# First three gated units by single row tile, in a fused layer-norm, spectral-filter and GEGLU kernel

## Chip, cores and metric

The kernel runs on one core of a Trainium2 chip. The time is the device time of one launch in microseconds (us), and the median of several runs counts; lower is better.

## Reference

```python
def _A_ref(x, w_r, w_i):                      # global spectral filter
    X = jnp.fft.rfft2(x.astype(jnp.float32), axes=(-2, -1))
    return jnp.fft.irfft2(X * (w_r + 1j * w_i), s=(S, D), axes=(-2, -1)).astype(jnp.bfloat16)

def _B_ref(x, w_gate, w_up, w_down):          # GEGLU, tanh gelu
    h = _gelu(x @ w_gate) * (x @ w_up)
    return h @ w_down

xn = _layernorm(A_x)                          # (1, 2048, 512) bf16, eps 1e-5
return A_x + _A_ref(xn, A_w_r, A_w_i) + _B_ref(xn, B_w_gate, B_w_up, B_w_down)
```

The gate and up weights are 512 x 1792, the down weights 1792 x 512, all bf16. The input B_x is not used.

## The kernel before

The 2048 rows are 16 tiles of 128 partitions; tile j holds the rows 16p + j. Four tiles make a block of 512 rows. Two branches share the normalized rows `xn`.

**The normalization.** `ln_stats(j)` (L410) takes the mean and variance of a tile on DVE (VectorE), in two instructions, statistics and aggregate. For the first two tiles `ln_sqrt` (L416) takes the root on ACT (ScalarE) and `ln_recip` (L420) the reciprocal on DVE; for the others `ln_rstd` (L425) does both on POOL (GpSimd). `ln_apply(j)` (L433) writes the normalized tile on DVE. Between tiles 0 and 1 nothing is split: one root and one reciprocal serve both.

**Transposes.** PE (TensorE) contracts over partitions, so the gated branch needs `xnT`, the rows transposed, in four chunks of 128 features. `transposes_by_tile(0, 2, ring_sp)` (L439) does the eight 128 x 128 transposes of tiles 0 and 1 and copies each chunk of 256 rows, in turn on DVE and ACT. `transposes` (L461) does two or four tiles at once in the same way; the last two blocks use DMA transposes (`transfers`, L488).

**The gated branch.** `geglu_unit(b, fc, a, w, ring)` (L529) makes 128 of the 1792 hidden features for w rows of block b from row a: four gate matmuls, four up matmuls, gelu on ACT out of the gate's PSUM bank, and the product on DVE out of the up bank into `hT`. There are 14 units to a block. Each unit takes two PSUM banks from a ring (`ring_first` has six, `ring_gu` three). A bank comes free when gelu or the product has read it. `down_unit` (L577) does the down projection of one tile.

The first units of block 0 are made in two passes: units 0 to NHALF - 1 for rows 0 to 255 first, then the same for rows 256 to 511; the rest have all 512 rows. All matmuls of one engine are in program order.

**The spectral branch** goes by `half_fold` (POOL, L500), `mirror_fold` (DVE, L507), `unit_A` and `unit_d` (PE, L610 and L636), a shuffle through DRAM, `unit_B`, the filter product on DVE, `unit_c`, a second shuffle, `unit_e` and `unit_fin`. Its small matmuls alternate with gated and down units, which the code calls fillers (`filler`, L838). They are taken from one list in a fixed order.

**Order.** There is no planner: `_Sched` (L152) records each operation on its engine's list in the order in which the Python code calls it, with semaphores for what it depends on. Every engine runs its list strictly in order. An instruction of DVE that waits holds all DVE instructions behind it.

**Loads.** SP and ACT issue the DMAs. The gate and up weights come in five column pieces (`WPIECES`, L344), loaded by `load_w` (L348). One semaphore counts both loads of a piece, and the gate matmuls wait for it. Up weights of piece 0 are issued by ACT after the identity; SP issues x tiles 0 and 1, the gate weights of piece 0, x tiles 2 and 3, pieces 1 and 2, and then the rest. `warm_up` (L519) runs matmuls on zeros at the start, 46 with no wait but that for the zeros, and 4 after the first reciprocal.

Of the kernel before, what the change touches and what calls it, by code (L numbers as in the profile page):

```python
# [7 lines left out]
ACT = mybir.ActivationFunctionType  # L8
# [6 lines left out]
HD = 256  # L15
NK = 257
FF = 1792
P = 128
NJ = 16
NG = 32  # L20
NDC = 4
NFC = 14
NGG = 3
NX1 = 4
NWARM = (46, 4)
LN_EPS = 1e-5


# [123 lines left out]
class _Sched:  # L152
# [14 lines left out]
    def total(self, stream):  # L167
        return (stream, self.stream_cnt[stream])
# [59 lines left out]
def bass_parallel_sum__spectral_gfnet__glu_gated_geglu__prompt_kernel(  # L228
# [15 lines left out]
    xv = A_x.rearrange("b (p j) d -> p (b j) d", j=NJ)  # L244
# [3 lines left out]
    sch = _Sched()  # L248

    with ExitStack() as es:  # L250
# [4 lines left out]
        x_sb = sb("x_sb", [P, NJ, D])  # L255
        xnT = sb("xnT", [P, NDC, S])
        wg_sb = sb("wg_sb", [P, NDC, FF])
        wu_sb = sb("wu_sb", [P, NDC, FF])
# [26 lines left out]
        xn = bufA[:, :].rearrange("p (j c) -> p j c", j=NJ)  # L285
# [12 lines left out]
        ident = small[:, 0:P]  # L298
# [20 lines left out]
        def sp_bank_bf(slot):  # L319
            return ps_bf[:, slot * 1024:(slot + 1) * 1024]  # L320
# [3 lines left out]
        ring_sp = _Ring((3, 4, 5, 6), bank_readers)  # L324
        ring_dn = _Ring((7,), bank_readers)

        ring_first = _Ring((0, 1, 2, 7, 5, 6), bank_readers)
        ring_tr = _Ring((3, 4), bank_readers)

        streams = [("pe", 1), ("act", 1), ("dve", 1), ("pool", 1)]  # L330
        streams += [(n, 16) for n in ("x0", "x1", "x2", "x3", "xc1", "xc2", "xc3", "ident", "small", "fa", "eg", "wd", "wr", "wi",
                                      "w0", "w1", "w2", "w3", "w4", "dr0", "dr1", "perm1", "jx0", "jx1", "jx2", "jx3", "vd0_0", "vd0_1", "vd0_2", "vd1_0", "vd1_1", "vd1_2", "vd2_0", "vd2_1", "vd2_2", "vd3_0", "vd3_1", "vd3_2", "perm2", "tr2", "tr3", "out")]
        for name, inc in streams:
            sem = es.enter_context(nc.semaphore("sem_" + name))
            sch.add_stream(name, sem, inc)
        total = sch.total

        def load(stream, dst, src, eng="sp"):
            sch.op(eng, lambda e: e.dma_start(dst, src), stream=stream)
            return total(stream)  # L340


        ev_id = load("ident", small[:, 0:P], c_small.ap()[:, 0:P], eng="act")
        WPIECES = ((0, 384), (384, 640), (640, 896), (896, 1280), (1280, FF))  # L344
        ev_w = {}
        spec = {}

        def load_w(i, which=(0, 1), eng="sp"):  # L348
            a, b = WPIECES[i]
            for q in which:  # L350
                dst, src = ((wg_sb, B_w_gate), (wu_sb, B_w_up))[q]
                load("w%d" % i, dst[:, :, a:b], src[:, a:b].rearrange("(r p) f -> p r f", p=P), eng=eng)
            ev_w[i] = total("w%d" % i)

        def load_xc(m):
            ev = load("xc%d" % m, x_sb[:, 4 * m:4 * m + 4, :], xv[:, 4 * m:4 * m + 4, :])
# [1 line left out]
                ev_x[j] = ev  # L358

        ev_x = {}  # L360
        load_w(0, (1,), eng="act")
        for j in range(4):
            ev_x[j] = load("x%d" % j, x_sb[:, j, :], xv[:, j, :])
            if j == 1:
                load_w(0, (0,))
        load_w(1)
        load_w(2)
        load_xc(1)
# [41 lines left out]
        def ln_stats(j):  # L410
            ev = sch.op("dve", lambda e: e.bn_stats(st[:, j, :], x_sb[:, j, :]), deps=[ev_x[j]])  # L411
            ev_ag[j] = sch.op("dve", lambda e: e.bn_aggr(ag[:, j, :], st[:, j, :]), deps=[ev])  # L412
# [3 lines left out]
        def ln_sqrt(a, b):  # L416
            return sch.op("act", lambda e: e.activation(rstd[:, a:b], ag[:, a:b, 1], ACT.Sqrt, bias=eps_t[:], scale=1.0),
                          deps=[ev_ag[b - 1], ev_eps])

        def ln_recip(a, b, ev):  # L420
            ev = sch.op("dve", lambda e: e.reciprocal(rstd[:, a:b], rstd[:, a:b]), deps=[ev])
            for j in range(a, b):
                ev_rstd[j] = ev
# [7 lines left out]
        ev_xn = {}  # L431

        def ln_apply(j):  # L433
            ev_xn[j] = sch.op("dve", lambda e: e.tensor_scalar(xn[:, j, :], x_sb[:, j, :], ag[:, j, 0:1], rstd[:, j:j + 1],  # L434
                                                             ALU.subtract, ALU.mult), deps=[ev_rstd[j], ev_ag[j]])

        ev_xnT = {}

        def transposes_by_tile(a, b, ring):  # L439

            n = (b - a) * P
            slots = [ring.alloc(1) for _ in range(NDC)]
            banks = [sp_bank_bf(slot)[:, 0:n] for slot, _ in slots]
            evs = []
            for j in range(a, b):
                for r in range(NDC):
                    ev_t = sch.op("pe", lambda e, j=j, r=r: e.transpose(banks[r][:, (j - a) * P:(j - a + 1) * P], xn[:, j, r * P:(r + 1) * P], ident),
                                  deps=[ev_id, ev_xn[j]] + slots[r][1])
                    if j < b - 1:
                        continue  # L450
                    dst = xnT[:, r, a * P:b * P]
                    if r % 2 == 0:
                        ev = sch.op("dve", lambda e, dst=dst, r=r: e.tensor_copy(dst, banks[r]), deps=[ev_t])  # L453
                    else:
                        ev = sch.op("act", lambda e, dst=dst, r=r: e.activation(dst, banks[r], ACT.Copy), deps=[ev_t])
                    ring.add_reader(slots[r][0], ev)
                    evs.append(ev)
            for j in range(a, b):
                ev_xnT[j] = evs

        def transposes(a, b, ring, per=2):  # L461

# [66 lines left out]
        def geglu_unit(b, fc, a=0, w=512, ring=None):  # L529

            k = geg["k"]
            geg["k"] = k + 1
            s2 = k % NGG
            hb = b % 2
            ring = ring or ring_gu
            evw = [ev_w[i] for i, (lo, hi) in enumerate(WPIECES) if lo < (fc + 1) * P and fc * P < hi]
            evx = [ev_xnT[4 * b + i] for i in range(a // P, (a + w) // P)]
            gslot, gdeps = ring.alloc(1)

            def mm(e, wsb, slot, dcs=range(NDC)):  # L540
                ins = None
                for dc in dcs:
                    ins = e.matmul(gu_bank(slot)[:, 0:w], wsb[:, dc, fc * P:(fc + 1) * P], xnT[:, dc, b * 512 + a:b * 512 + a + w],  # L543
                                   start=(dc == 0), stop=(dc == NDC - 1))
                return ins

            if b == 0 and fc == 0 and a == 0:
                for dc in range(NDC):
                    ev_gm = sch.op("pe", lambda e, dc=dc: mm(e, wg_sb, gslot, (dc,)), deps=evw + [x[dc] for x in evx] + gdeps)
            else:  # L550
                ev_gm = sch.op("pe", lambda e: mm(e, wg_sb, gslot), deps=evw + evx + gdeps)
            uslot, udeps = ring.alloc(1)
            ev_um = sch.op("pe", lambda e: mm(e, wu_sb, uslot), deps=udeps)
            gg = gg_sb[s2][:, 0:w]
            ev_gg = sch.op("act", lambda e: e.activation(gg, gu_bank(gslot)[:, 0:w], ACT.Gelu_apprx_tanh),  # L555
                           deps=[ev_gm] + gg_readers[s2])
            gg_readers[s2] = []
            ring.add_reader(gslot, ev_gg)
            hdeps = []
            if fc == 0 and a == 0:  # L560
                hdeps = list(hT_readers[hb])
                hT_readers[hb] = []
            ev_h = sch.op("dve", lambda e: e.tensor_tensor(hT[hb][:, fc, a:a + w], gu_bank(uslot)[:, 0:w], gg, ALU.mult),  # L563
                          deps=[ev_um, ev_gg] + hdeps)
            ring.add_reader(uslot, ev_h)
            gg_readers[s2].append(ev_h)
            ev_h_block.setdefault(b, []).append(ev_h)
# [227 lines left out]
            finished(j, ev_o)  # L795


        NHALF = 6
        ln_stats(0)
        ln_stats(1)  # L800
        ev_sq = ln_sqrt(0, 2)
        sch.op("act", lambda e: e.activation(warm[:], eps_t[:], ACT.Gelu_apprx_tanh), deps=[ev_eps])
        ln_recip(0, 2, ev_sq)
        for n, ev in zip(NWARM, (None, ev_rstd[0])):
            warm_up(n, ev)
        ln_apply(0)
        ln_apply(1)
        transposes_by_tile(0, 2, ring_sp)
        ln_stats(2)
        ln_stats(3)  # L810
        ln_rstd(2, 4)
        for fc in range(NHALF):
            geglu_unit(0, fc, 0, 256, ring_first)
            if fc == 1:
                ln_apply(2)
                ln_apply(3)
                half_fold(0)
            if fc == 3:
                transposes(2, 4, ring_tr)
        for fc in range(NHALF):  # L820
            geglu_unit(0, fc, 256, 256, ring_first)
# [16 lines left out]
        def filler(n=1):  # L838
            for _ in range(n):
                u = next(fill, None)  # L840
                if u is None:
                    return
                todo["left"] -= 1
                if u[0] == "g":
                    geglu_unit(u[1], u[2])
                else:
                    down_unit(u[1], u[2])

        filler()
        for j in range(4, 8):  # L850
            ln_apply(j)
        filler(2)
        transposes(4, 8, ring_tr)
        half_fold(1)
        filter_i = load_filter("wi", wi_sb, A_w_i)
# [104 lines left out]
```

## Time and profile before

| | |
|---|---|
| runs (us) | 180.08, 180.95, 181.80; median 180.95 |
| profiled execution | 180.17 us, span 178.4 us |
| PE busy | 174.7 us (98%) |
| DVE, ACT, POOL busy | 116.0, 86.5, 55.2 us |
| DMA | 27.15 MB, mean 152 GB/s |
| first gate matmul | at 7.14 us |
| second pass of block 0 begins | at 12.97 us |
| transposes of tiles 4 to 7 begin | at 23.39 us |

The span is the time from the first to the last instruction in the trace; the rest of the execution's time lies around it. A matmul's recorded duration holds the way through the array, so matmuls in a row overlap, and it is their distance from start to start that counts. "Idle before" and "<-" name who ended a wait. "ps" is PSUM, "bufA" the normalized rows, "bufC" the half folds.

### The profile page before, as it was taken

Reading aid. Unit: us, or ns where it says so; the run is one execution under the profiler, and the core shown is the slowest. Engines: PE = TensorE matmul, PEld = TensorE weight load, DVE = VectorE, ACT = ScalarE, POOL = GpSimd, SP = SyncE. Lnnn points to the kernel's source line nnn. Section 1 sums busy time; section 2 is a strip of 40 time slices with the busy share of each in tenths; the row PEclk is TensorE's granted clock in tenths of the full one; section 3 lists DMA queues with packets and bytes.
Section 4 is the critical chain, followed back from the end, with each engine's and each line's share of the span. In section 5 each row is a group of like instructions: output and inputs, shape, how many; then the busy total and the mean of one; then the engine's idle time right before and its main releaser. Section 6 shows DMA issues by size and latency. Waiting matters only on the chain.

```text
span 178.4 us, 3133 instructions
## 1 busy us (share of the span) xinstructions
PE 174.7 (98%) x1136; PEld 98.2 (55%) x1136; DVE 116.0 (65%) x250; ACT 86.5 (49%) x159; POOL 55.2 (31%) x54
## 2 busy tenths in 40 slices
PE   7999999999999999999999999999999999999994
PEld 7888465555555544454555555444455555555443
DVE  3768958798685628438586785954355868885731
ACT  2644357777362633066375764632173536662100
POOL 0073290373630000000000000000017869997760
PEclk9999999999999999999999999999999999999999
DMA  4999999999998693913435666744500111111101
GB/s 147 323 342 379 372 379 149 202 156 239 221 159 198 150 313 106 324 53 81 123 104 125 123 184 149 177 90 117 118 6 29 59 59 32 61 65 48 41 29 59
DMA packets 37520, 27.15 MB, mean 152 GB/s; under 512 B 6656, under 2 KB 36736, under 8 KB 37376
## 3 DMA queue, kind: packets, MB, share of 16 engines
q1 hardware_dynamic: 33664, 24.95, 55.1%
q10 hardware_dynamic: 3840, 2.00, 5.8%
q8 instruction: 9, 0.15, 0.4%
q14 instruction: 7, 0.06, 0.2%
HBM read 17.48 MB, written 6.30 MB: 133 GB/s over the span
## 4 chain that ended last, share of the span: by engine, by line
PE 87%; POOL 5%; DVE 5%; issue 1%
PE ps L543 48%; PE ps L589 25%; POOL bufC L504 5%; PE ps L524 3%; PE ps L722 2%; PE ps L753 2%; PE ps L774 2%; PE ps L691 2%; DVE bufA L434 2%; DVE hT L563 1%; PE ps L616 1%; PE ps L642 1%; PE ps L473 1%; DVE bufB L509 1%; POOL rstd L427 1%
## 5 line engine op out<-in xcount | busy, mean ns | idle before, releaser
L543 PE MATMUL ps<-xnT,wg_sb 128*128 128x512 bf16 (+1 forms) x248 | 58.5, 359 | 0.3 <-DVE xnT L453 0.3
L543 PE MATMUL ps<-xnT,wu_sb 128*128 128x512 bf16 (+1 forms) x248 | 58.6, 359 | 0.0
L563 DVE TENSOR_TENSOR hT<-ps,gg 128x512 bf16<-128x512 f32 (+1 forms) x62 | 39.3, 637 | 23.2 <-PE ps L543 21.6
L589 PE MATMUL ps<-wd_sb,hT 128*128 128x512 bf16 (+2 forms) x238 | 50.7, 367 | 0.0
L555 ACT ACTIVATE gg<-ps 128x512 bf16<-128x512 f32 (+1 forms) x62 | 34.4, 555 | 25.2 <-PE ps L543 23.6
L788 POOL TENSOR_TENSOR bufC<-bufC 128x256 bf16<-128x256 f32 x16 | 14.7, 919 | 86.5 <-DVE bufC L785 86.5
L543 PEld LDWEIGHTS ps<-xnT,wu_sb 128*128 128x128 bf16 x248 | 24.2, 98 | 24.2
L589 PEld LDWEIGHTS ps<-wd_sb,hT 128*128 128x128 bf16 x238 | 22.4, 98 | 23.2
L543 PEld LDWEIGHTS ps<-xnT,wg_sb 128*128 128x128 bf16 x248 | 23.0, 98 | 15.4 <-issue 0.5
L600 DVE TENSOR_TENSOR x_sb<-ps,x_sb 128x512 bf16<-128x512 f32 (+2 forms) x17 | 11.2, 660 | 23.9 <-PE ps L589 23.9
L792 POOL TENSOR_TENSOR x_sb<-x_sb,bufC 128x512 bf16<-128x512 bf16 x16 | 18.7, 1169 | 2.3
L504 POOL TENSOR_TENSOR bufC<-bufA 128x1024 bf16<-128x1024 bf16 x8 | 16.8, 2124 | 7.9 <-DVE bufA L434 7.9
L758 ACT ACTIVATE bufA<-ps 128x512 bf16<-128x512 f32 x16 | 9.4, 597 | 16.9 <-PE ps L753 16.9
L727 ACT ACTIVATE Vp<-ps 128x514 bf16<-128x514 f32 x16 | 9.5, 599 | 15.4 <-PE ps L722 15.4
L650 ACT ACTIVATE bufB<-ps 128x512 bf16<-128x512 f32 x16 | 11.9, 743 | 9.5 <-PE ps L642 9.5
L411 DVE BATCH_NORM_STATS2 st<-x_sb 128x6 f32<-128x512 bf16 x16 | 10.9, 678 | 2.2 <-DMA x_sb<-in_A_x_dram 2.2
L784 DVE TENSOR_TENSOR bufC<-bufC,ps 128x256 f32<-128x256 f32 x16 | 6.7, 421 | 5.3 <-ACT bufC L781 5.3
L696 ACT ACTIVATE Xc<-ps 128x514 bf16<-128x514 f32 x12 | 7.0, 595 | 1.0 <-PE ps L691 1.0
L623 ACT ACTIVATE tmp<-ps 128x512 bf16<-128x512 f32 x9 | 5.4, 597 | 4.4 <-PE ps L616 4.4
L426 POOL TENSOR_SCALAR rstd<-ag 128x4 f32<-128x4 f32 (+1 forms) x4 | 1.3, 316 | 19.9 <-DVE ag L412 19.9
L781 ACT ACTIVATE bufC<-ps 128x256 f32<-128x256 f32 x16 | 6.0, 378 | 2.6 <-PE ps L774 2.6
L788 DVE TENSOR_TENSOR bufC<-bufC 128x256 bf16<-128x256 f32 x16 | 6.8, 425 | 0.5
(50 smaller groups left out, 138.0 us busy)
## 6 DMA issues: line engine op xcount, KB each, us to landing
stage_g<-Vp SPq DMA_DIRECT2D x16, 128.5 KB, 3.1
bufC<-stage_p SPq DMA_DIRECT2D x4, 512.0 KB, 5.5
out_dram<-x_sb SPq DMA_DIRECT2D x15, 128.0 KB, 1.8
wd_sb<-in_B_w_down_dram SPq DMA_DIRECT2D x1, 1792.0 KB, 14.8
stage_p<-bufB SPq DMA_DIRECT2D x7, 256.0 KB, 5.6
wr_sb<-in_A_w_r_dram SPq DMA_DIRECT2D x6, 257.0 KB, 10.8
wi_sb<-in_A_w_i_dram SPq DMA_DIRECT2D x6, 257.0 KB, 10.0
JX<-Xc SPq DMA_DIRECT2D x24, 64.2 KB, 2.3
```

What stands on the lines that cost most here:

```text
L411: ev = sch.op("dve", lambda e: e.bn_stats(st[:, j, :], x_sb[:, j, :]), deps=[ev_x[j]])
L504: ev_hf[m] = [sch.op("pool", lambda e, t=t, op=op: e.tensor_tensor(half[:, m, t, :, :], rows[:, 0, :, :], rows[:, 1, :, :], op), deps=deps ...
L543: ins = e.matmul(gu_bank(slot)[:, 0:w], wsb[:, dc, fc * P:(fc + 1) * P], xnT[:, dc, b * 512 + a:b * 512 + a + w], start=(dc == 0), stop=(d ...
L555: ev_gg = sch.op("act", lambda e: e.activation(gg, gu_bank(gslot)[:, 0:w], ACT.Gelu_apprx_tanh), deps=[ev_gm] + gg_readers[s2])
L563: ev_h = sch.op("dve", lambda e: e.tensor_tensor(hT[hb][:, fc, a:a + w], gu_bank(uslot)[:, 0:w], gg, ALU.mult), deps=[ev_um, ev_gg] + hdeps)
L589: ins = e.matmul(bank(slot)[:, 0:w], hT[hb][:, fc, jj * P:(jj + 1) * P], wd_sb[:, fc, cs], start=(fc == 0), stop=(fc == NFC - 1))
L600: ev_a = sch.op("dve", lambda e, slot=slot, cs=cs, w=w: e.tensor_tensor(x_sb[:, j, cs], bank(slot)[:, 0:w], x_sb[:, j, cs], ALU.add), deps ...
L650: ev_T[j] = sch.op("act", lambda e: e.activation(dst, src, ACT.Copy), deps=[ev_p])
L727: ev_v = sch.op("act", lambda e: e.activation(Vp[sv][:], sp_pair(slot), ACT.Copy), deps=[ev_p] + Vp_readers[sv])
L758: ev_ZT[j] = sch.op("act", lambda e: e.activation(ZT[:, :, j, :], src, ACT.Copy), deps=[ev_p] + [ev_xnT[i][0] for i in (11, 15)])
L788: y = [sch.op(("dve", "pool")[h], lambda e, h=h, op=op: e.tensor_tensor(rS[s2][:, h * HD:(h + 1) * HD], yeS[s2][:, 0, :], yeS[s2][:, 1, :] ...
L792: ev_o = sch.op("pool", lambda e: e.tensor_tensor(x_sb[:, j, :], x_sb[:, j, :], rS[s2], ALU.add), deps=[a, b, ev_xn[j]] + ev_acc.get(j, []))
```

## The change

The layer norm's root and reciprocal are taken for tile 0 and tile 1 apart. Tile 0 is transposed and copied on DVE (two pairs of chunks) before tile 1 is applied on DVE; tile 1 is transposed after unit 0 of tile 0 and copied on ACT. Units 0 to 2 are made for tile 0 alone, then for tile 1 alone; units 3 to 6 for both. The second pass has seven units. Gate and up weights have semaphores of their own, and up matmuls wait for theirs. Tile 1's load goes to ACT's queue, both loads of piece 0 to SP's ahead of tiles 2 and 3. The statistics of tiles 2 and 3 follow the products of the narrow units. There are 40 and 3 warm-up matmuls. One filler instead of two stands between the application of tiles 4 to 7 and their transposes.

```diff
-NWARM = (46, 4)
+NWARM = (40, 3)
...
+        streams += [("w%d%s" % (i, q), 16) for i in range(5) for q in "gu"]
...
-                load("w%d" % i, dst[:, :, a:b], src[:, a:b].rearrange("(r p) f -> p r f", p=P), eng=eng)
-            ev_w[i] = total("w%d" % i)
+                name = "w%d%s" % (i, "gu"[q])
+                load(name, dst[:, :, a:b], src[:, a:b].rearrange("(r p) f -> p r f", p=P), eng=eng)
+                ev_w[i, q] = total(name)
...
-        load_w(0, (1,), eng="act")
-        for j in range(4):
+        for j, eng in ((0, "sp"), (1, "act")):
+            ev_x[j] = load("x%d" % j, x_sb[:, j, :], xv[:, j, :], eng=eng)
+        load_w(0)
+        for j in (2, 3):
             ev_x[j] = load("x%d" % j, x_sb[:, j, :], xv[:, j, :])
-            if j == 1:
-                load_w(0, (0,))
...
+        def transpose_first(j, eng):
+            evs = []
+            for h in range(2):
+                slot, bdeps = ring_tr.alloc(1)
+                bank = sp_bank_bf(slot)[:, 0:HD].rearrange("p (r s) -> p r s", r=2)
+                def f_tr(e, h=h, bank=bank):
+                    ins = None
+                    for r in range(2):
+                        ins = e.transpose(bank[:, r, :], xn[:, j, (2 * h + r) * P:(2 * h + r + 1) * P], ident)
+                    return ins
+                ev_t = sch.op("pe", f_tr, deps=[ev_id, ev_xn[j]] + bdeps)
+                dst, src = xnT[:, 2 * h:2 * h + 2, j * P:(j + 1) * P], bank
+                if eng == "dve":
+                    ev = sch.op("dve", lambda e, dst=dst, src=src: e.tensor_copy(dst, src), deps=[ev_t])
+                else:
+                    ev = sch.op("act", lambda e, dst=dst, src=src: e.activation(dst, src, ACT.Copy), deps=[ev_t])
+                ring_tr.add_reader(slot, ev)
+                evs += [ev, ev]
+            ev_xnT[j] = evs
...
-            evw = [ev_w[i] for i, (lo, hi) in enumerate(WPIECES) if lo < (fc + 1) * P and fc * P < hi]
+            pieces = [i for i, (lo, hi) in enumerate(WPIECES) if lo < (fc + 1) * P and fc * P < hi]
+            evw, evw_up = ([ev_w[i, q] for i in pieces] for q in range(2))
...
-            ev_um = sch.op("pe", lambda e: mm(e, wu_sb, uslot), deps=udeps)
+            ev_um = sch.op("pe", lambda e: mm(e, wu_sb, uslot), deps=evw_up + udeps)
...
-        NHALF = 6
+        NQUARTER, NHALF = 3, 7
         ln_stats(0)
         ln_stats(1)
-        ev_sq = ln_sqrt(0, 2)
+        ev_sq = [ln_sqrt(j, j + 1) for j in range(2)]
         sch.op("act", lambda e: e.activation(warm[:], eps_t[:], ACT.Gelu_apprx_tanh), deps=[ev_eps])
-        ln_recip(0, 2, ev_sq)
+        ln_recip(0, 1, ev_sq[0])
         for n, ev in zip(NWARM, (None, ev_rstd[0])):
             warm_up(n, ev)
         ln_apply(0)
+        ln_recip(1, 2, ev_sq[1])
+        transpose_first(0, "dve")
         ln_apply(1)
-        transposes_by_tile(0, 2, ring_sp)
+        for fc in range(NQUARTER):
+            geglu_unit(0, fc, 0, P, ring_first)
+            if fc == 0:
+                transpose_first(1, "act")
         ln_stats(2)
-        ln_stats(3)
+        for fc in range(NQUARTER):
+            geglu_unit(0, fc, P, P, ring_first)
+            if fc == 0:
+                ln_stats(3)
         ln_rstd(2, 4)
-        for fc in range(NHALF):
+        for fc in range(NQUARTER, NHALF):
             geglu_unit(0, fc, 0, 256, ring_first)
-            if fc == 1:
+            if fc == NQUARTER:
                 ln_apply(2)
                 ln_apply(3)
                 half_fold(0)
-            if fc == 3:
+            if fc == NHALF - 2:
                 transposes(2, 4, ring_tr)
         for fc in range(NHALF):
             geglu_unit(0, fc, 256, 256, ring_first)
...
         for j in range(4, 8):
             ln_apply(j)
-        filler(2)
+        filler()
         transposes(4, 8, ring_tr)
```

## The prediction

> **What bounds the kernel now.** I read the page's busy shares first, then the waits of TensorE, then the chain, then the timeline of the first 26 us, because the edit touches only those.
>
> ```profile
> span 178.4 us, 3133 instructions
> PE 174.7 (98%) x1136; PEld 98.2 (55%) x1136; DVE 116.0 (65%) x250; ACT 86.5 (49%) x159; POOL 55.2 (31%) x54
> ...
> PE 87%; POOL 5%; DVE 5%; issue 1%
> ...
> PE ps L524 <- DVE hT L405: 1.0, 1, 1.0
> PE ps L543 <- DVE xnT L453: 0.3, 1, 0.3
> ```
>
> The first two lines say that PE (TensorE) fills 98% of the span, the third that the chain which ends last runs mostly over it, the last two that PE waits visibly only twice, both before 7.2 us. So the time is the moment when gated matmuls begin, plus a nearly solid row of matmuls, plus each stall that the edit opens in it. A gain off PE is worth nothing; a PE start earlier by d is worth d if no later wait gives it back.
>
> ```profile
> L524 PE MATMUL ps<-hT x50: 219/314/315, 1.0 to 6.2; 128*128 128x128 bf16 x50
> L447 PE MATMUL ps<-small,bufA x8: 218/219/220, 6.2 to 6.6; 128*128 128x128 bf16 x8
> ...
> 4.67 0.18 DVE L412 BATCH_NORM_AGGREGATE ag<-st 128x2 f32<-128x6 f32 x1
> 4.89 0.29 ACT L417 ACTIVATE rstd<-ag,eps_t 128x2 f32<-128x2 f32 x1 [1.86 <-DVE ag L412]
> 5.21 0.17 DVE L421 RECIPROCAL rstd<-rstd 128x2 f32<-128x2 f32 x1 [0.36 <-ACT rstd L417]
> 5.42 0.73 DVE L434 TENSOR_SCALAR bufA<-x_sb,ag,rstd 128x512 bf16<-128x512 bf16 x2
> 6.22 0.61 PE L447 MATMUL ps<-small,bufA 128*128 128x128 bf16 x8
> 6.70 0.49 DVE L453 COPY xnT<-ps 128x256 bf16<-128x256 bf16 x2 [0.55 <-PE ps L447]
> 7.14 0.62 PE L543 MATMUL ps<-xnT,wg_sb 128*128 128x256 bf16 x4 [0.31 <-DVE xnT L453]
> ...
> 8.62 0.18 DVE L412 BATCH_NORM_AGGREGATE ag<-st 128x2 f32<-128x6 f32 x1
> 9.97 0.74 DVE L434 TENSOR_SCALAR bufA<-x_sb,ag,rstd 128x512 bf16<-128x512 bf16 x2 [0.39 <-POOL rstd L427]
> 10.76 0.62 PE L473 MATMUL ps<-small,bufA 128*128 128x128 bf16 x8
> ...
> 20.51 0.69 DVE L563 TENSOR_TENSOR hT<-ps,gg 128x512 bf16<-128x512 f32 x1
> 21.11 1.37 DVE L434 TENSOR_SCALAR bufA<-x_sb,ag,rstd 128x512 bf16<-128x512 bf16 x4
> 23.39 1.06 PE L473 MATMUL ps<-small,bufA 128*128 128x128 bf16 x16
> ```
>
> The warm-up matmul of L524 takes 314 ns and the transpose of L447, of the same shape, 219: PE runs at half pace until about 6.1 us, though the page's row of granted clock shows 9 throughout. Fifty of them in 5.41 us start 0.107 apart. Next, the head: statistics of two tiles, root, reciprocal, both tiles applied, eight transposes, copies, first gate matmul at 7.14. Then two places that the edit shifts: the transposes of tiles 2 and 3 at 10.76 and of tiles 4 to 7 at 23.39. At 23.39 the operands were ready at 21.11 + 1.37 = 22.48, 0.9 us early.
>
> **Start, -0.69 us.** Now the root is taken per tile. DVE's aggregate of tile 1 starts at 4.67; the next DVE instruction followed an aggregate by 0.10 elsewhere (8.62, then 8.72), and tile 0's root is done by 4.4 (its aggregate starts at 3.88, + 0.18 + 0.04 + 0.29), so reciprocal at 4.77, application 4.97 to 5.38. PE has 43 warm-ups, 0.97 + 43 x 0.107 = 5.57, which is later, so the four transposes of tile 0 start at 5.57, still slow: first pair done 5.57 + 0.107 + 0.314 = 5.99, second 6.20. DVE copies pairs of 128x256 (0.29, 0.21 apart): 6.03 to 6.32 and 6.24 to 6.53. The first gate matmul came 0.14 after its copy before; so 6.46 instead of 7.14, rounded to -0.69. Ends: -0.97, if full pace came before 5.4 (transposes 5.42 to 5.70, copy to 6.03, gate 6.17); -0.5 if the small DVE steps space like the root's 0.36 wait.
>
> **Moved behind the start, +0.27.** Tile 1 is applied after tile 0's two copies on DVE (6.44 to 6.85), and its four transposes stand on PE between units 0 and 1: 4 x 0.056 = 0.22 that lay before 7.14. PE has unit 0 to do until 6.93, so it doesn't wait. The second pair of the first gate waits about 0.05 for the second copy (0 to 0.15).
>
> **Narrow matmuls, +0.07.** Three units for two tiles are 48 matmuls of 128 columns instead of 24 of 256. L447's eight, each with its own weights, take 0.61 - 0.22 = 0.39 for seven pitches, 56 ns; the 256 wide take (0.60 - 0.27)/3 = 109. So 48 x 56 - 24 x 109 = 0.07 (0.05 to 0.10). Unit 6, now in two halves, adds 8 x (2 x 109 - 217) = 0.01. The Trainium skill speaks against this part: "TensorE: Matmul & The Clock Gate", section "Back-to-back issue gap", gives some 81 ns for each 128-column matmul in a stream with weight loads. By that the part would cost 48 x 0.081 - 24 x 0.109 = 1.27 us, an estimate; L447's row has 56, and I go by the row.
>
> **PSUM wait, +0.14.** In this stretch DVE has two statistics (0.72 to the aggregate, 0.10 after) and six products. A product of 256 columns takes 0.41, one of 512 0.69, so about 0.28 for 128, every 0.22. Gelu likewise 0.28 (0.38 and 0.60). ACT now copies tile 1's transposes first (7.3 to 7.96), so unit 1's gelu starts at 7.86 and its product at 8.17, unit 2's at 8.39; statistics of tile 2 run from 8.61, then unit 0's second product at 9.43, statistics of tile 3 from 9.65, aggregate 10.37, unit 1's second product 10.47 to 10.75. Unit 4's up matmul needs that bank (six banks, three units) and PE is there at 10.68: with 0.07 for the release, 10.82. Bounds 0 and 0.3.
>
> **Tiles 2 and 3, +0.27.** Their aggregate ends the statistics 1.75 later than before (10.37 against 8.62), because they queue behind products on DVE. From aggregate to application it was 9.97 - 8.62 = 1.35 on POOL; so applications 11.72 to 12.46, transposes at 12.51. PE has finished units 3, 4, 5 at 12.13: a wait of 0.38, where before it was 0.11 (10.65 to 10.76). Ends: -0.11 if DVE is quick, 0.6. Half fold 0 on POOL follows, 1.7 later, and is needed only by the mirror folds near 20.5. The second pass then starts 0.07 later than the same work did before (-0.69 + 0.27 + 0.08 + 0.14 + 0.27): before, with unit 6 added, 12.97 + 0.87 = 13.84; now 13.91. The head start is gone.
>
> **Tiles 4 to 7, +0.48.** Seven units in the first pass move one filler: the four applications stand behind unit 7's product with only unit 8 as cover, where it was units 7 and 8 behind unit 6's product. The second pass ends at 13.91 + 7 x 0.873 = 20.02 (a unit of 256 columns is 8 x 0.109), so unit 7 is issued until 21.75 (8 x 0.216), drained at 21.91, product 21.93, applications 0.60 after it (20.51 to 21.11), 1.37 long: 23.90, transposes at 23.95. Unit 8 ends at 21.75 + 1.73 = 23.48, so PE stands 0.48, counted with roundings (0.2 to 0.7; the mirror folds take 1.28 on DVE just before and may push the product). Later waits are measured from PE's own products (the chain's POOL parts begin at the product of 34.7), so they move with PE and give nothing back.
>
> **At nothing.** x1 goes to ACT's queue and the first up weights to SP's, 0.43 to 0.54 an issue, so tile 2's load is SP's fourth issue both times. Tile 1 landed at 3.7 and is read at 3.98; that slack of 0.2 covers it. The first gate weights landed at 1.64 + 4.8 = 6.4 behind the same bytes that now include the up weights; these are needed at 6.71. Waiting apart adds a wait before up matmuls, with all later PE work behind it; at the change of piece (unit 3, 9.78) the pitch was the usual 0.44. The seven warm-ups saved lie inside the start.
>
> **Sum:** -0.69 + 0.27 + 0.08 + 0.14 + 0.27 + 0.48 = +0.55. The profiled execution took 180.17, with 178.4 of span, so 180.72. Its time is 0.78 below the median of three, 180.95 (180.08 to 181.8). Taking two thirds of that distance, the base is 180.69 and the result 181.2. One per cent, 1.8 us, is about what a measurement of this kernel can tell from no change.
>
> **Rivals.** *The head start survives:* DVE keeps up and both transposes find their operands, so -0.69 + 0.27 + 0.08 - 0.11 = -0.45, 180.2. For it: DVE is idle 1.6 us among products in this window. Against it: the one-filler cover is shorter than the DVE steps by rows. Chance 0.22. *Half pace lasts:* PE idles 5.99 to 6.46, where it had an unbroken 5.17 us (0.97 to 6.14) before full pace. If the gap starts the count anew, full pace comes at 11.6: half of 5.17 lost, 2.6, of which the waits hide 0.3: 180.69 + 0.55 + 2.3 = 183.5. It decides for slower from 1.2 lost, full pace after 8.9. Against it: most of the stretch is filled. Chance 0.10. The same page of the skill, section "What's actually happening", has the clock follow free-running windows of 3.4 us; by it a missed window would end at 9.55 and cost some 1.5, an estimate, and the moment would differ from run to run. *The up weights bind:* last on SP's queue, they land like tile 3's load (2.55 + 4.5 = 7.1) instead of 6.4; up matmuls stand 0.4 and the sum is +0.95, 181.6. Against it: same bytes ahead. Chance 0.10. The forecast has 0.58, with a range of its own from 180.7 to 182.1 (sums from 0 to +1.4, without the corners where all ends meet).
>
> The range: the lowest sum of the ends, -0.97 + 0.27 + 0.06 - 0.11 + 0.2 = -0.55, gives 180.1; the highest, -0.5 + 0.37 + 0.11 + 0.3 + 0.6 + 0.7 = +1.58, gives 182.3. Few of them meet; with the rivals I take 180.2 to 182.5. Slower by over 1%: half pace and a little of the forecast, 0.12; faster 0.03, from a survived start on a low median; within 1% 0.85.
>
> **What would show it.** Right: first gate matmul near 6.5; the aggregate of tile 3 near 10.4; transposes of tiles 2 and 3 near 12.5 and of tiles 4 to 7 near 23.9, both with PE idle before them, the second about half a microsecond; from there each stage 0.5 later than before. Wrong: transposes of tiles 4 to 7 before 23.4; 128-column gate matmuls further apart than 60 ns after 6.5; gated matmuls at half pace beyond 7; up matmuls released by a DMA.

## The result, and the profile after

The changed kernel takes 182.80 us (median of 14 runs, 181.33 to 183.89), the kernel before 180.75 (14 runs). The ratio is 1.0106, with a 95% interval from 1.0073 to 1.0139: slower by about 2 us. The forecast was 181.2 with a range to 182.5, so the time lies outside it. The profiled execution took 182.73, with a span of 180.9.

From the page, the span, the busy time of PE and the shares of the chain:

```profile
span 180.9 us, 3205 instructions
PE 175.0 (97%) x1161; PEld 99.3 (55%) x1161; DVE 116.5 (64%) x255; ACT 87.5 (48%) x164; POOL 55.2 (31%) x54
...
PE 81%; DVE 8%; POOL 6%; DMA 2%; issue 1%; ACTq 0%
```

PE has almost the same busy time as before (174.7), in a span 2.5 longer: it waits more. The chain now has a DMA in it. In order of time, its longest early piece is this (start, length, what):

```profile
1.11 4.12 DMA x_sb<-in_A_x_dram
```

That is tile 1's load on ACT's queue. PE's waits say what hung on it (engine and line, released by: total us, times, longest):

```profile
PE ps L527 <- DVE rstd L423: 1.6, 1, 1.6
PE ps L527 <- DVE hT L407: 1.0, 1, 1.0
PE ps L476 <- DVE bufA L436: 0.5, 2, 0.4
PE ps L547 <- DVE xnT L457: 0.4, 1, 0.4
PE ps L451 <- DVE rstd L423: 0.2, 1, 0.2
```

The first is new and the longest: the second group of warm-ups stands 1.6 us for tile 0's reciprocal. The third is the two transposes of tiles 2 to 7 that the prediction named. The timeline shows how a load of tile 1 came to hold tile 0:

```profile
3.87 0.18 DVE L414 BATCH_NORM_AGGREGATE ag<-st 128x2 f32<-128x6 f32 x1
4.09 0.29 ACT L419 ACTIVATE rstd<-ag,eps_t 128x1 f32<-128x1 f32 x1 [1.10 <-DVE ag L414]
5.25 0.69 DVE L413 BATCH_NORM_STATS2 st<-x_sb 128x6 f32<-128x512 bf16 x1 [1.20 <-DMA x_sb<-in_A_x_dram]
6.08 0.13 DVE L423 RECIPROCAL rstd<-rstd 128x1 f32<-128x1 f32 x1
7.55 0.59 PE L547 MATMUL ps<-xnT,wg_sb 128*128 128x128 bf16 x4 [0.36 <-DVE xnT L457]
...
14.82 0.62 PE L476 MATMUL ps<-small,bufA 128*128 128x128 bf16 x8 [0.15 <-DVE bufA L436]
...
26.30 1.07 PE L476 MATMUL ps<-small,bufA 128*128 128x128 bf16 x16 [0.35 <-DVE bufA L436]
```

Tile 0's root is done at 4.38. Its reciprocal stands on DVE behind tile 1's statistics, which wait for the load until 5.25, so it starts at 6.08 instead of the 4.77 predicted. The first gate matmul comes at 7.55; before, it was 7.14. The transposes of tiles 4 to 7 start at 26.30 instead of 23.39.

There is a second loss. By stretches of time (us, PE busy and count, PEld, DVE, ACT, POOL; then the granted clock, DMA share, GB/s):

```profile
4.70:6.30 1.60, 0.03 (x1) 0.04 (x2) 0.97 (x4) 0.10 (x1) 0.00 (x0) 1.00 1.08 351
7.50:10.50 3.00, 2.95 (x29) 2.98 (x30) 1.01 (x4) 1.88 (x7) 0.00 (x0) 0.50 1.20 305
```

PE had reached full pace at 3.76, stood idle from 4.7 to 6.3, and was granted half the clock from 7.2 to 10.6, while the narrow units ran. From 7.61 to 10.49 it issued 27 matmuls, 0.107 apart; at full pace they are 0.056 apart, so 1.4 us were lost.

Added up to the start of the transposes of tiles 4 to 7, with the kernel that has the loads of before (first experiment) beside it:

| step, us against before | predicted | changed kernel | with old loads |
|---|---|---|---|
| first gate matmul | -0.69 | +0.41 | -0.59 |
| tile 1's transposes behind the start, wait for copies | +0.27 | +0.22 | +0.22 |
| narrow matmuls | +0.08 | +0.07 | +0.07 |
| PSUM wait | +0.14 | 0 | +0.05 |
| tiles 2 and 3, with the copies after | +0.27 | +0.27 | +0.35 |
| tiles 4 to 7 | +0.48 | +0.52 | +0.51 |
| half pace | none | +1.4 | none |
| sum | +0.55 | +2.9 | +0.61 |
| measured start of those transposes | | +2.91 | +0.64 |

(Each wait is the distance between neighbouring matmul starts over the usual one; narrow matmuls and tile 1's transposes are counted at full pace.) Of the 2.9 the rest of the kernel gives 0.4 back.

The 14 runs fall in two groups: six from 181.33 to 182.06 (mean 181.7) and eight from 182.73 to 183.89 (mean 183.3). Six of the eight have a mean granted clock of 0.991, as the profiled one has; the six of the lower group all have 1.000. The other two of the eight have 1.000 as well: this mean counts time without a clock record as full, so a first grant that comes late doesn't show in it (the profiled execution of e19 below is such a case). So a run without lasting half pace is about 0.9 over the kernel before, and lasting half pace adds about 1.6 in a good half of the runs.

### The profile page after: what moved, and what is told of

Read it like the earlier page. It is cut to its first block, busy times and chain, and to the rows that moved or that the text cites. A ratio compares the mean times of both kernels' runs of the same rounds, so it can differ in the third digit from the quotient of the medians.

```text
span 180.9 us, 3205 instructions
## 1 busy us (share of the span) xinstructions
PE 175.0 (97%) x1161; PEld 99.3 (55%) x1161; DVE 116.5 (64%) x255; ACT 87.5 (48%) x164; POOL 55.2 (31%) x54
## 4 chain that ended last, share of the span: by engine, by line
PE 81%; DVE 8%; POOL 6%; DMA 2%; issue 1%; ACTq 0%
PE ps L547 45%; PE ps L593 25%; POOL bufC L507 5%; DVE bufA L436 3%; DMA x_sb<-in_A_x_dram 2%; PE ps L726 2%; PE ps L778 2%; PE ps L757 2%; PE ps L695 2%; DVE hT L567 2%; DVE st L413 1%; PE ps L620 1%; PE ps L646 1%; POOL rstd L429 1%; PE ps L476 1%
## 5 line engine op out<-in xcount | busy, mean ns | idle before, releaser
L547 PE MATMUL ps<-xnT,wg_sb 128*128 128x512 bf16 (+2 forms) x264 | 59.9, 351 | 0.4 <-DVE xnT L457 0.4
L547 PE MATMUL ps<-xnT,wu_sb 128*128 128x512 bf16 (+2 forms) x264 | 60.0, 351 | 0.0
L567 DVE TENSOR_TENSOR hT<-ps,gg 128x512 bf16<-128x512 f32 (+2 forms) x66 | 39.7, 607 | 24.6 <-PE ps L547 22.9
L559 ACT ACTIVATE gg<-ps 128x512 bf16<-128x512 f32 (+2 forms) x66 | 35.1, 532 | 25.1 <-PE ps L547 23.8
L547 PEld LDWEIGHTS ps<-xnT,wu_sb 128*128 128x128 bf16 x264 | 25.7, 100 | 23.6
L547 PEld LDWEIGHTS ps<-xnT,wg_sb 128*128 128x128 bf16 x264 | 24.4, 100 | 15.0 <-issue 0.7
```

## Experiments

Times are compared with the kernel before in the same job, since its median went from 180.14 to 180.81 from job to job. "Over" means over that kernel's median.

**Old loads** (e1). Tile 1 back on SP's queue, the first up weights on ACT's.

```diff
-        for j, eng in ((0, "sp"), (1, "act")):
-            ev_x[j] = load("x%d" % j, x_sb[:, j, :], xv[:, j, :], eng=eng)
-        load_w(0)
-        for j in (2, 3):
+        load_w(0, (1,), eng="act")
+        for j in range(4):
             ev_x[j] = load("x%d" % j, x_sb[:, j, :], xv[:, j, :])
+            if j == 1:
+                load_w(0, (0,))
```

> The changed kernel with the loads of before (tile 1 on SP's queue ahead of the gate weights, the first up weights on ACT's queue), nothing else touched. Theory L (late tile 1: on ACT's queue its load took 4.1 us from issue instead of 2.6, tile 1's statistics start at 5.25 instead of 3.98, and tile 0's reciprocal is queued behind them on DVE): statistics of tile 1 back at 4.0, reciprocal of tile 0 near 4.8, first gate matmul near 6.5, no gap of over a microsecond in PE's warm-up, no second stretch at half pace; time 180.9 to 181.6, that is 1.2 to 1.9 under the changed kernel's 182.8. Theory N (the narrow units, the PSUM ring and the later transposes are what costs): at most 0.4 under the changed kernel, 182.4 or more.

180.56 against 180.14: 0.42 over, ratio 1.0020 (1.0003 to 1.0037), and only 0.5 between the fastest and slowest of 12 runs. From its timeline:

```profile
4.82 0.13 DVE L423 RECIPROCAL rstd<-rstd 128x1 f32<-128x1 f32 x1
6.55 0.40 PE L547 MATMUL ps<-xnT,wg_sb 128*128 128x128 bf16 x4 [0.62 <-DMA wg_sb<-in_B_w_gate_dram]
24.02 1.07 PE L476 MATMUL ps<-small,bufA 128*128 128x128 bf16 x16 [0.35 <-DVE bufA L436]
```

The reciprocal is where the prediction had it (4.77), and the wait before the last transposes is there. The first gate is near the predicted 6.46, but by another bound: full pace came at 4.8, tile 0's first copy began at 5.85 instead of 6.03, and PE then stood 0.62 for the gate weights. The loads cost the change 0.0086 of its 0.0106; theory L holds. The 0.42 that remain are about half of the 0.9 by which the lower group of the changed kernel's runs is over.

**New loads in the kernel before** (e2). The same edit the other way round.

> The kernel before with the loads of the change alone (tile 1 on ACT's queue, both first weights on SP's). Theory L: statistics of tile 1 at 5.2 instead of 3.98, so the shared root and both applications are 1.2 later, first gate matmul near 8.4 instead of 7.14, PE idle for a microsecond or more before it; time up by 1.0 to 1.5, and more where the pace drops again, 181.8 to 183.3. Theory N: no difference that can be told, 180.4 to 181.1.

181.19: 1.05 over (1.0034 to 1.0086). Tile 1's statistics start at 5.28 and the first gate comes at 8.26, 1.1 late, as expected. Two of its 12 runs (182.41 and 183.04) have a mean granted clock of 0.991, the others 1.000.

**Which load.** Tile 1 alone moved back (e16), the up weights alone moved back (e22), and the changed kernel again (e19), on one chip.

```diff
 # e16: tile 1 back on SP
-        for j, eng in ((0, "sp"), (1, "act")):
-            ev_x[j] = load("x%d" % j, x_sb[:, j, :], xv[:, j, :], eng=eng)
+        for j in (0, 1):
+            ev_x[j] = load("x%d" % j, x_sb[:, j, :], xv[:, j, :])
         load_w(0)
...
 # e22: up weights back on ACT, behind tile 1
-        load_w(0)
+        load_w(0, (1,), eng="act")
+        load_w(0, (0,))
```

> The changed kernel with tile 1's load alone moved back to SP's queue, ahead of the gate weights; the up weights stay on SP's queue behind them. Theory L (tile 1's load alone does it): statistics of tile 1 within 0.1 of the end of tile 0's, no gap of over 0.7 in PE's warm-up, first gate matmul 6.5 to 6.9; time 0.3 to 0.8 over the kernel before, 1.0 to 1.7 under the changed kernel beside it. Rival U (the up weights, now last, are what costs): up matmuls of unit 0 wait for a DMA for 0.5 or more and the time stays 1.2 or more over before.

> The changed kernel with the first up weights alone moved back to ACT's queue, behind tile 1, which stays there. Theory L: tile 1's statistics as late as in the changed kernel (5.0 to 5.4, or 0.2 earlier with less on SP's queue), first gate matmul near 7.5, half pace after it in a part of the executions; time within 0.4 of the changed kernel beside it, 1.5 to 2.1 over before. Rival U: time falls to 0.8 over before or less.

> The changed kernel itself, unaltered, beside the two others on the same chip, so that differences among them don't rest on two chips. Both theories: 1.5 to 2.3 over the kernel before, in two groups about 1.2 apart by whether full pace is taken back once early on.

Before 180.81 here. Tile 1 back on SP: 181.22 (0.9995 to 1.0043). Up weights back on ACT: 183.17 (1.0074 to 1.0154). Changed kernel: 183.21 (1.0066 to 1.0164). Tile 1's load alone makes the difference, and the up weights alone make none. The difference of 2.0 is more than the 1.0 to 1.7 expected, and e22 and e19, both 2.4 over, lie just above their ranges: in their profiles tile 1's statistics start later still (5.47 and 5.64), and five and four of their six runs are over 182.9. Rival U is still seen in a part: with both weights behind tile 1 on SP's queue, PE waits for them (e16).

```profile
6.18 0.40 PE L547 MATMUL ps<-xnT,wg_sb 128*128 128x128 bf16 x4 [0.38 <-DMA wg_sb<-in_B_w_gate_dram]
7.32 0.40 PE L547 MATMUL ps<-xnT,wu_sb 128*128 128x128 bf16 x4 [0.74 <-DMA wu_sb<-in_B_w_up_dram]
```

In the changed kernel there is no such wait: its up weights landed at 6.5, before its first gate at 7.55.

**Tile 0 ahead** (e5). The load stays late, but tile 0's root, reciprocal and application are called ahead of tile 1's statistics.

```diff
         ln_stats(0)
-        ln_stats(1)
-        ev_sq = [ln_sqrt(j, j + 1) for j in range(2)]
-        sch.op("act", lambda e: e.activation(warm[:], eps_t[:], ACT.Gelu_apprx_tanh), deps=[ev_eps])
+        ev_sq = [ln_sqrt(0, 1)]
         ln_recip(0, 1, ev_sq[0])
...
         ln_apply(0)
+        ln_stats(1)
+        ev_sq.append(ln_sqrt(1, 2))
+        sch.op("act", lambda e: e.activation(warm[:], eps_t[:], ACT.Gelu_apprx_tanh), deps=[ev_eps])
         ln_recip(1, 2, ev_sq[1])
         transpose_first(0, "dve")
```

> The changed kernel, loads untouched (tile 1 still late on ACT's queue), but on DVE and ACT tile 0's root, reciprocal and application are called ahead of tile 1's statistics; the gelu table is loaded after tile 1's root as before. Theory L says the harm of the late tile 1 goes through the order of DVE's queue: then reciprocal of tile 0 near 4.5 instead of 6.08, its application by 5.1, first gate matmul near 6.1 to 6.5 (bound by the gate weights), the PE gap ahead of it under 0.7 and no return to half pace, though tile 1's statistics still start at 5.0 to 5.3; unit 1's gelu and the rest 0.3 to 0.6 later than with the loads of before. Time 0.5 to 1.0 over the kernel before on the same chip, against 1.9 for the changed kernel. Rival (the late load does its harm through tile 1's own work, whose rows are needed soon after anyway): first gate near 6.5, but PE then stands over 1 us for tile 1's transposes, and the time is 1.3 to 1.9 over before.

181.54, 1.03 over (1.0037 to 1.0075): about half of the loss goes.

```profile
4.38 0.16 DVE L423 RECIPROCAL rstd<-rstd 128x1 f32<-128x1 f32 x1 [0.36 <-ACT rstd L419]
5.35 0.69 DVE L413 BATCH_NORM_STATS2 st<-x_sb 128x6 f32<-128x512 bf16 x1 [0.37 <-DMA x_sb<-in_A_x_dram]
7.12 0.39 PE L547 MATMUL ps<-xnT,wg_sb 128*128 128x128 bf16 x4 [0.96 <-DVE xnT L457]
```

Tile 0's reciprocal no longer waits for the late tile 1. But the first gate is at 7.12, not 6.1 to 6.5: I had left tile 0's copies behind tile 1's reciprocal on DVE, and that waits for the late tile too. DVE's order passes the delay on as long as anything of tile 1 stands ahead of something of tile 0. PE's longest gap once it has begun is the 0.96 before the first gate, and full pace, granted at 6.8 in this profile, lasts. At 1.03 over, the kernel is where the lower group of the changed kernel's runs is (0.9): what it shows to be gone is the lasting half pace; the 0.4 by which its first gate is earlier can't be seen in the time.

**Tile 1 first on ACT's queue**, ahead of the identity (e15).

> The changed kernel with one pair of issues exchanged: tile 1's load is ACT's first (0.73) and the identity's second (1.11). Theory L, with the queues taking turns packet by packet: tile 1's 128 KB then run beside tile 0's and ahead of most of the gate weights, its statistics start at 3.9 to 4.2 instead of 5.25, the first gate matmul comes near 6.5, no PE gap above 0.7 in the warm-up, and the time is 0.3 to 0.7 over the kernel before. Rival (ACT's queue as such is slow at the start, whatever stands in it first; there, 384 KB and 128 KB both landed 4.1 after issue): statistics of tile 1 at 4.6 or later and the time 1 or more over. A third outcome is that the identity is late now and holds the transposes.

181.60, 1.06 over (1.0040 to 1.0080). Tile 1's statistics follow tile 0's at once, as theory L has it, but tile 0's own came at 4.07 in this profile instead of 3.1, so tile 1's start at 4.89 and the first gate comes at 7.16. By its own signs (4.6 or later, 1 or more over) the rival fits, and theory L doesn't. Tile 1 took 3.5 from issue, tile 0 3.3. Whether two loads issued together hold each other up can't be said: tile 0 was also late (3.84 and 4.04) in two profiles of other kernels with different first loads. So it stays open why tile 1 is late on ACT's queue. In the changed kernel it landed at 5.23, beside the gate weights' 5.34, as sharing would have it; but in the kernel before the 384 KB of up weights in the same place took 4.1 as well, as a slow queue would have it.

**Sixty warm-ups** instead of 40 (e4).

> The changed kernel with 60 instead of 40 warm-up matmuls ahead of the reciprocal. In the changed kernel's profile PE was at full pace from 3.8 to 7.5, idle from 4.7 to 6.3, at half pace from 7.5 to 10.5. Theory H (that idle stretch is what takes the pace away): no return to half pace after the first gate matmul in executions where full pace came early, time 0.5 to 1.0 under the changed kernel, 181.8 to 182.3, with less spread; the first gate matmul stays near 7.5, because it hangs on tile 1. Rival (the pace falls whatever the warm-ups do): half pace again in about half of the executions and a median within 0.3 of the changed kernel, or above it where full pace comes late and 60 slow matmuls last to 7.4.

181.75, 1.61 over (1.0049 to 1.0111), with 1.15 between fastest and slowest and no return to half pace in the profile; the first gate stays at 7.56. All six runs have a mean granted clock of 1.000. So have all 24 runs of e1 and e16, where tile 1 isn't late; of the changed kernel's 20 runs (14 and e19's six) eight have 0.991, and of the 69 of the other kernels with tile 1 on SP's queue three have 0.99 (one each in e8, e10 and e14). It fits theory H, but 1.61 against the changed kernel's 2.05 falls just short of the 0.5 expected, and the intervals overlap, so the size of the effect rests on the two groups above.

**Two fillers** ahead of the transposes of tiles 4 to 7 (e3).

> The changed kernel with two fillers instead of one between the application of tiles 4 to 7 and their transposes. Theory L with the prediction's cover step: PE's wait of 0.52 before those transposes goes, nothing else moves, time 0.4 to 0.6 under the changed kernel, about 182.3. Rival: the wait comes back at the next place that hangs on these tiles (first products of block 1, or the wait for the fold at 55.9), and the time stays within 0.2 of the changed kernel.

183.61, 3.5 over (1.0159 to 1.0226): worse than the changed kernel, which neither theory had. The wait of 0.52 goes, and a worse one comes 100 us later. PE's wait (L757 is `unit_e`, behind the second shuffle), and the pace after it:

```profile
PE ps L757 <- DMA bufB<-stage_g: 2.0, 1, 2.0
...
131.00:135.00 4.00, 3.64 (x15) 1.79 (x16) 0.00 (x0) 1.68 (x3) 0.00 (x0) 0.57 0.02 4
```

The fillers come from one list. The unit taken early is missing as cover for the second shuffle through DRAM; PE stands 2 us for it and falls to half pace for 3.4 us.

**Old loads, two fillers, and none first in the spectral loop** (e8).

> The changed kernel with the loads of before, two fillers ahead of the transposes of tiles 4 to 7, and the first filler of the spectral loop left out, so that every later place has as many fillers left as in the changed kernel (moving one there alone took the cover from the second shuffle). Theory L: first gate near 6.5, no wait at the transposes of tiles 4 to 7 (0.51 with old loads alone) and none of 2 us at 129; time 0.1 under to 0.2 over the kernel before, against 0.42 over with old loads alone. Rival: the loop's first spectral unit now comes too soon after the transposes and waits for the fold or the copies, a new PE wait of 0.3 or more between 25 and 30, and the time stays 0.4 over.

181.28, 0.77 over (1.0019 to 1.0068). The rival came true: PE waits 0.6 us in the first spectral unit for a copy of the transposes. Its bank is the one that those transposes filled. Of the 2 us at the second shuffle 0.3 are left.

**Gate weights on ACT's queue (e9), and everything together (e10).**

> The changed kernel with tiles 0 and 1 on SP's queue, the first gate weights on ACT's queue and the first up weights third on SP's: the loads of before with gate and up exchanged. With the loads of before, PE waited 0.62 for the gate weights at 6.55. Theory: the gate weights land near 5.2, as the up weights did on ACT's queue, the first gate matmul comes at 6.1 to 6.4, and the wait moves to the up weights (0 to 0.2); time 0.1 to 0.4 over the kernel before. Rival (tile 1 sets the pace then: its application is queued behind tile 0's copies): first gate earlier, but the time no better than 0.4 over before.

> Everything together: gate weights on ACT's queue, tiles 0 and 1 on SP's, tile 0's root, reciprocal and application ahead of tile 1's statistics on DVE, two fillers ahead of the transposes of tiles 4 to 7 and none first in the spectral loop. Theory: first gate at 5.7 to 6.2, no wait of 0.5 near 23, the wait for tiles 2 and 3 of 0.4 stays; time 0.3 to 0.9 under the kernel before. Rival: the pairs of copies now wait behind tile 1's statistics on DVE, or full pace has not come by 6 and narrow units run at half pace; then within 0.2 of before.

181.06, 0.55 over (1.0017 to 1.0052), and 181.60, 1.09 over (1.0033 to 1.0092); both miss what was expected. In the first, the gate comes at 6.55 although the weights no longer hold it: here tile 0's copies do, and full pace came only at 6.0. The second has the copies behind tile 1's reciprocal again (first gate 6.81) and the spectral unit's wait of 0.6.

**Early applications, early statistics.** On old loads, the applications of tiles 4 to 7 are called ahead of the filler whose product they stood behind (e18); e12 also calls tile 2's statistics after unit 0's product and tile 3's ahead of the second products; e14 adds tile 0's chain ahead, its copies before tile 1's reciprocal, gate weights on ACT's queue, and 36 warm-ups.

```diff
-        filler()
         for j in range(4, 8):
             ln_apply(j)
-        filler()
+        filler(2)
         transposes(4, 8, ring_tr)
```

> The changed kernel with the loads of before, and the four applications of tiles 4 to 7 called ahead of the filler (unit 7) whose product they stood behind on DVE; the number of fillers at every place stays. Theory (the cover step of the prediction): applications start right after the mirror folds, near 21.5, and end by 23.0; PE's wait of 0.51 at the transposes goes; unit 7's product is 1.3 later on DVE, which nobody needs; time 0.4 to 0.6 under the changed kernel with the loads of before, that is 0.1 under to 0.1 over the kernel before. Rival: unit 7's late product holds a PSUM bank of the three and unit 9 waits as long, no gain.

> As the kernel with early applications, and in addition the statistics of tile 2 called right after unit 0's first product and those of tile 3 before the second products, so that they don't queue behind them on DVE. Theory: aggregate of tile 3 near 9.6 instead of 10.3, applications of tiles 2 and 3 by 11.8, the wait of 0.39 before their transposes gone or under 0.1; time 0.7 to 1.0 under the changed kernel with the loads of before, 0.3 to 0.6 under the kernel before. Rival: products of the narrow units come later on DVE and PE waits for PSUM banks instead; within 0.2 of before.

> As e12, and tile 0's chain (root, reciprocal, application) ahead of tile 1's statistics, tile 0's copies right after those, gate weights on ACT's queue and up weights on SP's, 36 warm-ups instead of 40. Theory: transposes of tile 0 at 5.2, copies from 5.9, first gate matmul at 6.2 to 6.4, tile 1 applied by 7.0; time 0.4 to 0.9 under the kernel before. Rival: the earlier start meets half pace (full pace came between 3.8 and 6.9 so far) or the up weights, and it is no better than e12.

Against 180.54: 180.60 (0.9974 to 1.0019), 180.36 (0.9980 to 1.0020) and 181.01 (1.0009 to 1.0043). The first two are as fast as the kernel before and no faster, the third is 0.47 slower; e12 and e14 were expected to be faster. The cover step is confirmed: with early applications, the transposes start at 23.55 with no wait. At the second shuffle PE waits 0.5 in e18's profile and not in e1's. But the changed kernel waits there too when it is run again, with the same fillers (e18, then e19):

```profile
PE ps L757 <- DMA bufB<-stage_g: 0.5, 1, 0.5
...
PE ps L757 <- DMA bufB<-stage_g: 0.4, 1, 0.4
```

So this wait differs from execution to execution, and that the earlier transposes bring it on isn't shown. The profiled execution of e12 was the slowest of its runs, so its waits for both shuffles (0.9 and 0.4) are not typical; the third kernel's profile shows half pace again. No version that I ran beats the kernel before.

## Why the prediction was wrong

**The step that failed is "At nothing"**, its sentence that tile 1 "landed at 3.7 and is read at 3.98; that slack of 0.2 covers it". I took its landing time over from SP's queue, where its 128 KB had only tile 0 ahead of them, to ACT's queue, where they ran beside the gate weights. They landed 4.1 after issue instead of 2.6, and the step cost 1.3 us on DVE and 1.1 at the first gate (7.55 against 6.46). That moving this load alone brings the loss and takes it away is shown (e16 against e19); whether the gate weights beside it or ACT's queue as such made it late is not (e15).

**Half pace** was among the rivals, at 0.10 and 183.5. It came, by another gap: not the 0.5 us after tile 0's transposes but the 1.6 that the late tile opened in the warm-ups. Its price was also too high: full pace came back at 10.6 rather than 11.6, so 1.4 were lost in the profile instead of 2.3. I priced the rivals apart; here one delay made the gap that made the other.

**The up weights** as a bound (0.10) aren't seen in the changed kernel, where they landed at 6.5, about as the step had it. With tile 1 ahead of them on the same queue (e16) they landed at 7.3, and PE waits 0.74, where I had 0.4.

**What held:** with old loads, the sum of the steps: +0.55 against +0.61 at the last transposes, and 0.42 in the time. The two DVE queue waits were sized within 0.1. The start's -0.59 is right in part by luck: copies and full pace came earlier than reckoned, and the gate weights, which the prediction's own row lets land at 6.4, became the bound. The PSUM wait was 0.05 instead of 0.14. Narrow matmuls were costed from the transposes' row (56 ns); in the old-loads kernel four of them take 0.39 with 0.22 for the last, 57 apart. The Trainium skill's 81 ns ("TensorE: Matmul & The Clock Gate", "Back-to-back issue gap") is not seen here.

**The claim that later waits give nothing back** is not quite right: of the 0.64 at the last transposes the span of e1 keeps 0.3 (178.7 against 178.4), and of the changed kernel's 2.9 it keeps 2.5. And e3 shows the second shuffle's wait depending on how much PE work is left ahead of it, not on PE's start alone.

**The direction** was a small loss within 1%; the measured loss is at 1.06% just beyond it.

## What to carry to other kernels

A landing time belongs to a load in its place: when a load changes its queue, or the loads beside it change, cost it anew from what now runs beside it, and take no slack from the old place. Then follow the in-order engine that reads it, because everything called behind that read is late too, also what doesn't need the data. When an early unit of cover is moved, look for the last place that drew on the same list.

## What the runs showed of the hardware

**Two queues share unevenly.** Tile 1 and the gate weights were issued 0.06 us apart on two queues. In the changed kernel, from 3.5 to 4.5 us (packets, MB, share of the engines; q10 is ACT's queue, q1 SP's):

```profile
q1 hardware_dynamic: 339, 0.25, 76.8%
q10 hardware_dynamic: 126, 0.11, 33.0%
```

ACT's queue got 0.11 of 0.36 MB. In the kernel before, with the up weights on ACT's queue, the same microsecond went almost wholly to it (440 packets, and 11 of SP's). The Trainium skill ("DMA: Bandwidth & Descriptors", section "Queues, rings and completion order", on arbitration) has each DMA engine take turns between queues packet by packet, a packet being several descriptors. The profile's packets are smaller (0.25 MB in 339 is 0.74 KB, about one row of the weight piece, 768 bytes), so these counts show the shares and don't test the turns. The first case agrees in that neither queue stops; in the second SP's hardly moved, and the trace doesn't say whether its gate weights, issued at 1.64, were ready to.

**The clock moves in steps of 3.4 us.** In the changed kernel's trace full pace lasts from 3.76 to 7.17 and half pace from there to 10.58, 3.41 each. In e3 half pace lasts from 131.51 to 134.92, 3.41 as well. In another execution of the changed kernel (e19) full pace came only at 10.0, after a gap from 5.4 to 6.6; its trace has no clock record, but the distance of its matmuls shows it (0.106 apart in the first line, 0.056 in the second):

```profile
9.27 0.63 PE L547 MATMUL ps<-xnT,wg_sb 128*128 128x128 bf16 x4
...
10.10 0.39 PE L547 MATMUL ps<-xnT,wg_sb 128*128 128x128 bf16 x4
```

So an idle stretch can cost in two ways: full pace is taken back, or it comes later; for e19 that the gap did it is inferred. The skill's page on TensorE ("What's actually happening") has such free-running windows of 3413 ns; these runs agree, and a gap of 1.6 us in one was enough. What a window of 3.41 needed to keep full pace can be narrowed down from PE's busy time in it: with 1.44 (e3, from 128.10), 1.63 (changed kernel, from 3.76) and 1.87 (e14, from 4.64) it was taken back, with 1.92 (e3, from 5.22) and 2.14 (e2, from 5.71) it was kept.
